# Attention and phase-mixing kernel: 64-column transposes without staging copies, the end of batch 0 in token pieces, batch 3's loads behind one gate, and a channel product ahead of each theta

## The chip, the core and the metric

The kernel runs on one core of one Trainium2 chip. A core has five engines with instruction streams of their own: PE (TensorE: matrix products and transposes into PSUM), DVE (VectorE), ACT (ScalarE), POOL (GpSimd, which here only issues loads) and SP (SyncE, which here issues stores and transposing DMAs). They wait for one another through semaphores; each runs its own instructions in order. Sixteen DMA engines move the data.

The metric is the time of one execution on the device in microseconds. Before the change it is 174.78 us, the median of six runs (174.43 to 175.14).

## The reference

Inputs are q, k, v of shape (4, 8, 768, 64) in float32 (batch, heads, tokens, head width) and the weights of a mixing layer. Reduced to what is computed:

```python
scores = q @ k.T / sqrt(64)
keep   = (pos_k < 8) | ((0 <= rel) & (rel < 96))      # rel = pos_q - pos_k
scores = where(keep, scores - slope[h] * dist, -1e9)  # dist = rel, or 96 for far global keys
x      = softmax(scores) @ v                          # heads side by side: (4, 768, 512)

theta  = x @ w_theta
y      = w_tok_r @ (x * cos(theta)) + w_tok_i @ (x * sin(theta))   # over tokens
u      = x + y
out    = u + relu(u @ w_ch)                            # over channels
```

Every token attends to the eight first ("global") tokens and to the 96 latest ones.

## The kernel before

**Tiles.** 768 tokens are six tiles of 128 (`NT`), 512 channels four groups of 128 (`NC`), eight heads four pairs (`NP`). A pair's two heads of width 64 fill the 128 partitions of qT and kT; their score products use 64 rows of the array each (L295). A pair has three chunks of scores, two key tiles each; each key tile meets its own and the next query tile. The eight global keys are kept by copying them over the first columns of a second key tensor, kG (`kglob`, L214), and likewise vG for v (`vglob`).

**One batch.** (1) Loads: q, k (`qk`) and v (`vn`) from HBM, cast to bf16 by POOL's DMAs. (2) q and k are transposed to qT and kT. Batches 0, 1 and 2 do it on PE, from `qkn`, a copy of qk in which the two heads of a pair lie side by side, so that six transposes of 128 columns make one PSUM tile, which ACT (kT) or DVE (qT) copies out. The copies into qkn are `cast0` (L198, batch 0) and `prep_copy` (L229, batches 1 and 2). Batch 3 does it with transposing DMAs from SP (`prep_dma`), for which its q and k are loaded token-wise, one DMA a head (L82). (3) `scores` and `score_exp` (L302): exp on ACT; the bias is a PE product in batch 0 (`score_bias`) and a product with a table, `etab`, on DVE in the others. (4) `values` (L352) makes x of a pair, with a reciprocal and a multiply on DVE (L360, L362), and `xtrans` makes xT: on PE in batch 0, with an SP DMA (L366) in the others. (5) `theta` (L389) needs all four groups of xT; sine and cosine on ACT (L395), zr and zi on DVE (L398, `zri`). (6) `mix` (L409): 12 products of 512 columns a token tile, then u on DVE (L414). (7) `utrans` makes uT (PE in batch 0 and for the last tile, SP's DMA at L423 else), and `chan` (L434) is four products, one DVE instruction for o_sb (L440) and a store.

**Order.** Batch 0's attention and theta are written out by hand for PE, DVE, ACT, POOL and SP (`manual_schedule`, from L504 to L575). After it, `weave` lays batch b's mixing and batch b+1's attention into one another by weights; in batch 0 the side work, whose first pieces are the transposes of batch 1, begins after 0.3 of the mixing. From there a planner orders each engine's instructions by its own costs, mostly as written; anchors (`behind`) keep the side work from running ahead. The last tile of batch 3 is by hand again.

**Where batches meet.** `order` (L587) holds what runs between two batches: the first four half-steps of theta (`th[:4]`), two of the channel products left from the batch before, `th[4:]`, the rest. Theta's half-steps take channel groups 0 to 2 first and group 3 last.

**Load queue.** POOL issues, in this order: batch 0 (pair 1, half of v, pairs 2 and 3, the other half), the weights, batch 1's q, k, v, batch 2's q, k and, in the weave, v; then the first four heads of batch 3, and behind a one-element copy that waits for the last xT of batch 1 (`load_behind`, L457) its other four heads and its v. The qk and vn buffers are two each, so batch 2 reuses batch 0's and batch 3 batch 1's.

The softmax here doesn't subtract the row's maximum and nothing guards it: scores larger than these inputs give would overflow.

## Time and profile before

| Quantity | Value |
|---|---|
| Median of six runs | 174.78 us (174.43 to 175.14) |
| The profiled execution, its own time | 174.41 us |
| Span of its instructions | 172.4 us |
| Instructions | 3627 |
| HBM read, written | 25.69 MB, 6.29 MB |
| DVE copies into qkn, batches 1 and 2 (L229) | 16, 340 ns each |
| PE transposes from qkn (L204, L244) | 48 and 96, of 128 columns |
| First product of mixing (L409) | 33.04 us |
| Gate of batch 3's loads (L457) | 73.02 us |

Times within the profile count from the start of the span. PE's busy share is no measure of its work: a product of 512 columns is shown with some 380 ns, though the next one starts 216 ns later. Busy shares are averages over stages with different limits; which wait ends last in a stage is read from the chain of work that ended last, which is followed back from the last instruction through what released each one. A row of a timeline gives start, length, engine, line, operation, written and read tiles, and in brackets the idle time before it with what ended it.

### The profile page before, as it was taken

What the parts mean: (1) busy time and instruction counts of PE and PEld (TensorE: products, weight loads), DVE (VectorE), ACT (ScalarE), POOL (GpSimd) and SP (SyncE); (2) the same over time, 40 slices, a digit from 0 to 9 for tenths busy, and PEclk for the clock granted to TensorE, in tenths of its full rate; (3) what the DMA queues carried; (4) which work ended last, traced back from release to release, by engine and by line L of the source; (5) the groups of instructions that cost most, each with busy time, mean ns of one, the idle gap of its engine ahead of it and who ended that gap; (6) DMA issues with size and microseconds to landing.
All of it is one profiled execution on the core that took longest, in us unless ns stands there. A gap on an engine that the chain in (4) does not pass through costs nothing.

```text
span 172.4 us, 3627 instructions
## 1 busy us (share of the span) xinstructions
PE 159.3 (92%) x1457; PEld 84.7 (49%) x1482; DVE 127.7 (74%) x288; ACT 99.1 (58%) x124; POOL 37.4 (22%) x45
## 2 busy tenths in 40 slices
PE   6789878999999999999999998999999989999991
PEld 1355655455755566544454563444554634444440
DVE  7578965678999999998587587597786838724443
ACT  2479676999497595489834730989348318500010
POOL 8974456005371010099000000000000000000000
PEclk9999999999999999999999999999999999999999
DMA  4999999999999999799999797787138571323335
GB/s 157 184 193 178 211 207 209 205 204 171 160 204 175 167 156 165 124 94 157 214 143 111 158 161 165 137 152 223 30 76 116 133 171 41 142 41 102 100 93 183
DMA packets 75088, 25.92 MB, mean 150 GB/s; under 512 B 63168, under 2 KB 72128, under 8 KB 75072
## 3 DMA queue, kind: packets, MB, share of 16 engines
q0 software_dynamic: 45680, 12.45, 78.9%
q1 hardware_dynamic: 28976, 12.72, 34.4%
q10 hardware_dynamic: 416, 0.52, 0.9%
q8 instruction: 11, 0.18, 0.4%
q14 instruction: 5, 0.04, 0.1%
HBM read 25.69 MB, written 6.29 MB: 186 GB/s over the span
## 4 chain that ended last, share of the span: by engine, by line
PE 49%; DMA 22%; DVE 19%; POOL 5%; issue 2%; ACT 1%; SPq 0%; DVEq 0%; POOLq 0%
PE ps L409 27%; DMA qk<-in_k_dram 11%; PE ps L434 9%; DMA w_nat<-in_moe_w_tok_r_dram 7%; PE pb L295 4%; PE pb L352 3%; PE pb L389 3%; DVE qT L249 3%; POOL qk L73 3%; DVE e L312 2%; PE ps L389 2%; DVE qkn L229 2%; DVE o_sb L440 2%; POOL vn L88 2%; DMA kT<-qk 2%
## 5 line engine op out<-in xcount | busy, mean ns | idle before, releaser
L409 PE MATMUL ps<-zri,w_tokT 128*128 128x512 bf16 x271 | 67.4, 380 | 1.5 <-issue 0.5
L302 ACT ACTIVATE e<-pb 128x1024 bf16<-128x1024 f32 (+1 forms) x48 | 43.6, 958 | 22.4 <-PE pb L295 22.2
L409 PEld LDWEIGHTS <-w_tokT 128*128 128x128 bf16 x288 | 26.1, 98 | 29.0 <-issue 1.0
L414 DVE TENSOR_TENSOR u<-x_sb,ps 128x512 bf16<-128x512 bf16 x24 | 16.4, 682 | 14.6 <-PE ps L409 12.7
L434 PE MATMUL ps<-w_ch_bf,uT 128*128 128x512 bf16 x94 | 23.9, 379 | 0.3 <-DVE u L414 0.2
L398 DVE TENSOR_TENSOR zri<-x_sb,cs 128x512 bf16<-128x512 bf16 x48 | 17.9, 417 | 8.0 <-ACT cs L395 7.7
L440 DVE SCALAR_TENSOR_TENSOR o_sb<-ps,u 128x512 f32<-128x512 f32 (+1 forms) x25 | 16.5, 661 | 3.1 <-PE ps L434 3.1
L395 ACT ACTIVATE cs<-pb,halfpi 128x1024 bf16<-128x1024 f32 x8 | 8.9, 1115 | 15.8 <-PE pb L389 15.8
L312 DVE TENSOR_TENSOR e<-e,etab 128x1024 bf16<-128x1024 bf16 (+1 forms) x24 | 14.7, 615 | 3.4 <-ACT e L302 3.4
L295 PE MATMUL pb<-qT,kT 64*128 64x128 bf16 x224 | 15.9, 223 | 0.8 <-ACT kT L211 0.3
L389 PE MATMUL pb<-w_theta_bf,xT 128*128 128x512 bf16 x62 | 15.0, 379 | 1.2 <-DMA xT<-x_sb 1.1
L295 PEld LDWEIGHTS <-kT 64*128 64x128 bf16 x224 | 9.0, 95 | 14.2 <-issue 13.0
L389 PEld LDWEIGHTS <-xT 128*128 128x128 bf16 x96 | 9.1, 98 | 12.0 <-DMA xT<-x_sb 2.1
L428 ACT COPY uT<-ps 128x512 bf16<-128x512 bf16 x7 | 4.1, 587 | 18.6 <-PE ps L427 18.6
L352 PEld LDWEIGHTS <-e 128*128 128x128 bf16 x352 | 12.7, 97 | 3.2 <-issue 1.2
L434 PEld LDWEIGHTS <-uT 128*128 128x128 bf16 x96 | 8.9, 98 | 10.0 <-ACT uT L428 0.3
L88 POOL DMA_DIRECT2D vn<-in_v_dram x5 | 9.6, 1928 | 11.9 <-DVE vn L68 10.3
L295 PE MATMUL pb<-qT,kG 64*128 64x128 bf16 x128 | 12.0, 221 | 0.3 <-DVE kG L220 0.3
L362 DVE TENSOR_TENSOR x_sb<-pb,rec 128x768 bf16<-128x768 f32 x12 | 11.4, 948 | 0.3
L315 DVE TENSOR_TENSOR e<-e,etab 128x1024 bf16<-128x1024 bf16 x12 | 8.2, 684 | 2.8 <-ACT e L302 2.8
L352 PE MATMUL pb<-vn,e 128*128 128x65 bf16 x168 | 9.6, 193 | 0.2 <-DVE x_sb L362 0.2
L251 ACT COPY kT<-ps 128x768 bf16<-128x768 bf16 x8 | 6.4, 798 | 5.0 <-PE ps L244 5.0
(74 smaller groups left out, 205.3 us busy)
## 6 DMA issues: line engine op xcount, KB each, us to landing
out_dram<-o_sb SPq DMA_DIRECT2D x23, 256.0 KB, 2.4
vn<-in_v_dram POOLq DMA_DIRECT2D x3, 768.0 KB, 22.8
qk<-in_q_dram POOLq DMA_DIRECT2D x2, 768.0 KB, 20.8
qk<-in_k_dram POOLq DMA_DIRECT2D x2, 768.0 KB, 23.4
w_nat<-in_moe_w_tok_r_dram POOLq DMA_DIRECT2D x3, 384.0 KB, 13.9
w_nat<-in_moe_w_tok_i_dram POOLq DMA_DIRECT2D x3, 384.0 KB, 14.9
vn<-in_v_dram POOLq DMA_DIRECT2D x2, 384.0 KB, 8.9
qk<-in_q_dram POOLq DMA_DIRECT2D x8, 96.0 KB, 9.0
```

Source lines behind the costliest of these rows:

```text
L88: nc.gpsimd.dma_start(out=vn[:, h0:h0 + n, :, 0:D].rearrange("p h t d -> p (h t) d"), in_=v[b, h0:h0 + n].rearrange("h (t p) d -> p (h t) ...
L295: nc.tensor.matmul(pb[:, hh, o:o + T], lhsT=lhsT, rhs=qT[R, (own, nxt)[part]], start=bool(b), stop=bool(b) or (jt == NT - 1 or (j == 1 and ...
L302: ins = nc.scalar.activation(e_c, pb[:, :, 0:n], AF.Exp, scale=scale).ins
L312: nc.vector.tensor_mul(e_c, e_c, tab[:, :, s0:s0 + n // T].rearrange("p a s n -> p a (s n)"))
L352: nc.tensor.matmul(o, lhsT=l_, rhs=r_, start=(i_ == 0), stop=(i_ == len(mms) - 1))
L362: nc.vector.tensor_mul(xv, po4[:, :, :, 0:D], rec.to_broadcast([T, n, NT, D]))
L389: nc.tensor.matmul(pb[j_] if last else pb[:, j_, :], lhsT=xT[:, dc, st(j_)], rhs=w_theta_bf[:, dc, :], start=(dc == 0), stop=(dc == NC - 1))
L398: nc.vector.tensor_mul(zri[b][:, i_, 2 * c + j_, :].rearrange("p (g d) -> p g d", g=NP), xb[:, :, 2 * c + j_, :], cs[:, i_, j_].rearrange( ...
L409: anchor["pe"] = nc.tensor.matmul(ps, lhsT=w_tokT[wi][:, st, tt * T:(tt + 1) * T], rhs=zri[b][:, wi, st, :], start=(st == 0 and wi == 0), ...
L414: anchor["dve"] = nc.vector.tensor_add(u_sb[b, tt].rearrange("p (g d) -> p g d", g=NP), x_sb[b][:, :, tt, :], ps.rearrange("p (g d) -> p g ...
L434: nc.tensor.matmul(ps_c, lhsT=uT[:, dc, :], rhs=w_ch_bf[:, dc, :], start=(dc == 0), stop=(dc == NC - 1))
L440: nc.vector.scalar_tensor_tensor(o_sb[:, cols], in0=ps_c[:, cols], scalar=0.0, in1=u[:, cols], op0=ALU.max, op1=ALU.add)
```

## The change

- Transposes of q and k on PE (`turn`): each head by itself, 64 stationary columns into 64 of the PSUM partitions, straight from qk; twelve in the place of six. The copies of batches 1 and 2 and of batch 0's pairs 1 to 3 go; pair 0 is still cast from float32, into a buffer `qk0`.
- Batch 0 by hand: the bias products of chunks 0 and 1 and one of the eight exp tables stand ahead of the first transposes; pair 0's kG is made on ACT in two pieces; chunk 2 of the scores stands ahead of the values of the pair before; the values and xT of the last pair are made for token tiles 0 to 3 and then 4 and 5; channel groups 0 to 2 of two thetas run before its last xT. `load_qk(0, 4, 2)` stands ahead of the first half of v.
- Batch 3: all eight heads and v are loaded behind the gate.
- `order`: one `chan` ahead of theta, one (in batch 1's case a `utrans`) in the middle, the rest behind.
- The last `chan` writes two PSUM tiles of 256 columns, so that the first half can go on while the second is computed.

```diff
     load_qk(0, 2, 2)
+    load_qk(0, 4, 2)
     load_v(0, 0, 4)
-    load_qk(0, 4, 2)
...
+    def turn(ps, src):
+        for t_ in range(NT):
+            for hh in range(2):
+                nc.tensor.transpose(ps[hh * D:(hh + 1) * D, t_, :], src[:, hh, t_, :], ident)
 
     def turn0(p, i_):
-        qkn = tiles0[p, "n"]
         ps = tiles0[p, i_] = ps_small([T, NT, T], BF)
-        for t_ in range(NT):
-            nc.tensor.transpose(ps[:, t_, :], qkn[:, t_, i_].rearrange("p h d -> p (h d)"), ident)
+        turn(ps, loads[0][0][:, i_, 2 * p:2 * p + 2] if p else qk0[:, i_])
...
-    def prep_copy(b, p):
-        qk = loads[b][0]
-        qkn = qkns[b, p] = att.tile([T, NT, 2, 2, D], BF, name="qkn", bufs=2)
-        with behind("dve"):
-            for i_ in range(2):
-                nc.vector.tensor_copy(
-                    out=qkn[:, :, i_].rearrange("p t h d -> p h t d"), in_=qk[:, i_, 2 * p:2 * p + 2])
-
-    def prep(b, p):
-        if p == 0:
-            prep_copy(b, 0)
-        if p + 1 < NP:
-            prep_copy(b, p + 1)
-        qkn = qkns[b, p]
+    def prep(b, p):
+        qk = loads[b][0]
...
             with behind("pe"):
-                for t_ in range(NT):
-                    nc.tensor.transpose(ps[:, t_, :], qkn[:, t_, i_].rearrange("p h d -> p (h d)"), ident)
+                turn(ps, qk[:, i_, 2 * p:2 * p + 2])
...
     def theta(b, c, j):
+        last0 = [(j_, NC - 1) for j_ in range(2)]
+        part = {0: [(0, dc) for dc in range(NC - 1)],
+                1: [(1, dc) for dc in range(NC - 1)] + last0,
+                2: [(j_, dc) for j_ in range(2) for dc in range(NC - 1)],
+                3: last0}[j]
...
     def chan(b, tt):
         u, uT = u_sb[b, tt], uTs[(b, tt)]
+        parts = 2 if (b, tt) == (B - 1, NT - 1) else 1
+        n = DM // parts
+        pss_c = [ps_small([T, n], FP) for _ in range(parts)]
+        for i_, ps_c in enumerate(pss_c):
+            for dc in range(NC):
+                nc.tensor.matmul(ps_c, lhsT=uT[:, dc, :], rhs=w_ch_bf[:, dc, i_ * n:(i_ + 1) * n],
+                                 start=(dc == 0), stop=(dc == NC - 1))
...
         with tc.issue_after(g):
-            load_qk_tokens(b, H // 2, H // 2)
+            alloc_qk(b)
+            load_qk_tokens(b, 0, H)
             load_all_v(b)
...
+    score_bias(0, 0)
+    score_bias(0, 1)
+    cast0(1, dve, 0)
+    bias_table(0)
+    cast0(1, act, 1)
     turn0(0, 1)
...
+    kglob(0, 0, 0, 1, act)
     score_mms(0, 0, 0)
-    score_mms(0, 0, 1)
+    kglob(0, 0, 1, NT - 2, act)
     score_exp(0, 0, 0)
...
+        score_bias(p, 2)
+        score_mms(0, p, 2)
         if p:
             values(0, p - 1, 0)
             values(0, p - 1, 1)
-        score_bias(p, 2)
-        score_mms(0, p, 2)
...
+    sine_table()
+    xtrans(0, p - 1, dve)
+    values(0, p, 0, 0, 4)
+    values(0, p, 1, 0, 4)
+    trans_w(0, act)
+    theta(0, 0, 2)
+    xtrans(0, p, dve, 0, 4)
+    values(0, p, 0, 4, 6)
+    values(0, p, 1, 4, 6)
+    theta(0, 1, 2)
+    xtrans(0, p, dve, 4, 6)
+    theta(0, 0, 3)
+    theta(0, 1, 3)
+    theta(0, 2, 2)
+    theta(0, 2, 3)
+    for h in range(1, H):
+        bias_table(h)
...
-        order = th[:4] + rest[:2] + th[4:] + rest[2:] if b else []
+        order = rest[:1] + th[:4] + rest[1:2] + th[4:] + rest[2:] if b else []
...
         if b == 0:
             side[:0] = [(0, lambda: load_all_v(2))]
-            side.append((0, lambda: (alloc_qk(3), load_qk_tokens(3, 0, H // 2))))
```

## The prediction, made before the changed kernel was run

> **What bounds the kernel now.** I read the engine totals first, then the chain of work that ended last in order of time, then each engine's timeline around the places that the diff touches.
>
> ```profile
> PE 159.3 (92%) x1457; PEld 84.7 (49%) x1482; DVE 127.7 (74%) x288; ACT 99.1 (58%) x124; POOL 37.4 (22%) x45
> ```
>
> PE looks full, but its ends are modelled, so I count its work from start to start. In the timeline a 512-column product takes 0.216 us, a 128-column transpose 0.056, a 65-column values product 0.029, and two row-tile score products (heads 0 and 1) start together and take 0.057 as a pair.
>
> ```profile
> 9.39 12.42 DMA w_nat<-in_moe_w_tok_r_dram
> ...
> 22.09 19.42 DMA qk<-in_k_dram
> 41.53 0.60 DVE qkn L229 x2
> ...
> 68.23 0.61 DVE u L414
> ...
> 68.88 1.02 PE ps L434 x4
> 69.90 0.34 PE ps L244 x6
> ```
>
> This is the chain, with columns start, length, what. Three regimes stand in it. Until 41.53 us it is the load queue: batch 1's k lands then, and no earlier engine work can move it. From 41.53 to 68.8 the chain is VectorE without a gap: batch 1's attention and batch 2's transposes inside batch 0's mixing. From 68.88 it is TensorE, apart from short waits at each batch's theta. PE's own demand in 41.5 to 68.9, counted from the weight loads of each line at the prices above, is 22.7 us, and 26 changes of tile shape at 0.09 (next fence) make 25.1 of 27.4 us: PE is idle for only 2.3 us there. So VectorE bounds that stretch, but PE is the next bound close behind.
>
> ```profile
> 80.03 1.02 PE L409 MATMUL ps<-zri,w_tokT 128*128 128x512 bf16 x4
> 80.98 0.34 PE L295 MATMUL pb<-qT,kT 64*128 64x128 bf16 x6
> ...
> 81.39 0.22 PE L295 MATMUL pb<-qT,kG 64*128 64x128 bf16 x2
> 81.54 0.82 PE L409 MATMUL ps<-zri,w_tokT 128*128 128x512 bf16 x3
> ```
>
> Columns: start, length, engine and line. Four mix products from 80.03 should end their issue at 80.89; the row-tile products start at 80.98. The last row-tile pair from 81.39 should be through at 81.45; mixing starts at 81.54. So each change between the full array and row tiles costs 0.09 us.
>
> **The copies go, the transposes double.** Batches 1 and 2 lose the copies into qkn:
>
> ```profile
> L229 DVE COPY qkn<-qk 128x768 bf16<-128x768 bf16 x16 | 5.0, 340 | 0.0
> ```
>
> Thirteen of the sixteen start in 41.5 to 68.9 and hold the chain for about 0.27 us each: 3.5 us off VectorE, which then needs 23.9 of 27.4 us and stops being the bound. In exchange each of the 16 PSUM tiles gets 12 transposes with 64 stationary columns, not 6 with 128. No row of before is column-tiled. Lower bound: the two heads run side by side as the row-tile pairs do, 6 x 0.056 = 0.34 us, nothing added. Upper bound: one after the other, 12 x 0.056 = 0.67 us, 0.34 more a tile. To both come changes of tile shape: putting column tiles where the transposes stand in the timeline adds nine pairs of changes (two neighbours are row-tile scores already), 9 x 0.19 = 1.7 us. [...] The row on the other side: 65-column products with a full 128-column load each issue every 0.029 us, so today's loads are hidden completely[...]. By the row the stretch needs 25.1 + 1.7 = 26.8 of 27.4 us on PE[...]. I take the row, as the nearest measured tiling, and allow 1.2 us of idle PE instead of 2.3, since chains of copies remain: 28.0 against 27.4, **+0.6 us**.
>
> **Batch 0 by hand.** The six casts of its pairs 1 to 3 (L198, 0.27 to 0.35 us each) leave VectorE; three blocks of column tiles add 3 x 0.19 = 0.56 us to PE. Scores of chunk 2 now stand ahead of the values of the pair before, which should return most of the ACT waits at 15.85, 20.57 and 24.36 (0.28, 1.19, 0.85 us): estimate 1.2 us. At the end the values of the first four token tiles need only chunks 0 and 1, and six products each of two thetas run before the last xT; from the last exp (25.17) to the first mix product (33.04) it is 7.87 us today, and ACT's sines pace what follows: estimate 0.9 us. The two extra reciprocals and multiplies fall into VectorE's 2.32 us wait before 30.93; without it they would cost about 0.8. The start is near zero: the four bias products (0.43 each, 6.82 to 8.66) move into PE's 1.63 us idle, but hold the first transposes to about 6.2 instead of 5.56, and kG's copies go to ACT, idle for 1.85 us; between -0.5 and +0.6, I take 0. The early bias_table(0), 0.7 us on ACT from 4.4, delays ACT's cast (5.00) by 0.1 and shortens the later run of eight tables; the earlier pair-2 load puts v behind 384 KB, with vG at 13.26 leaving 2.7 us after v's landing at 10.6. Both are nothing. Together mixing starts 1.2 - 0.56 + 0.9 = 1.5 us earlier. But the transposes of batch 1 wait for k at 41.53, where PE already waits 0.14 us. Only mix products that the planner pulls ahead of that wait keep the gain; unknown, between 0 and 1.5, I take half, **-0.7**.
>
> **Theta.** One chan (4 x 0.216 = 0.86 us) now stands in front.
>
> ```profile
> 105.06 1.46 PE L389 MATMUL pb<-w_theta_bf,xT 128*128 128x512 bf16 x6
> 107.16 2.33 PE L389 MATMUL pb<-w_theta_bf,xT 128*128 128x512 bf16 x10 [0.64 <-DMA xT<-x_sb]
> ...
> 114.06 1.02 PE L409 MATMUL ps<-zri,w_tokT 128*128 128x512 bf16 x3 [0.25 <-DVE o_sb L440]
> ...
> 139.20 1.46 PE L389 MATMUL pb<-w_theta_bf,xT 128*128 128x512 bf16 x6
> 141.15 2.33 PE L389 MATMUL pb<-w_theta_bf,xT 128*128 128x512 bf16 x9 [0.48 <-DMA xT<-x_sb]
> ```
>
> Six products from 105.06 are issued by 106.36, the seventh starts at 107.16: 0.80 us lost waiting for xT; from 139.20 the same reading gives 0.65. Both are under 0.86, and the uT needed was issued at 132.32 for the later one, so chan covers them whole. Its o_sb (0.61 us on VectorE) also leaves the row of zri products that PE waits for before 114.06 (0.41 from start to start). Sum **-1.85**. Batch 1's theta waits for nothing and gains nothing; were a chan late, it would hold theta by that much.
>
> **Batch 3's loads.** Eight q/k issues (L82, 0.83 us each) move from 46.12 to 62.8 behind the gate:
>
> ```profile
> 73.02 0.21 POOL L457 COPY gate<-xT 1x1 bf16<-1x1 bf16 x1 [10.19 <-DMA xT<-x_sb]
> ...
> 79.99 2.27 POOL L88 DMA_DIRECT2D vn<-in_v_dram  x1
> 84.22 5.91 SPq L423 DMA_TRANSPOSE uT<-u x2
> DMA to landing us min/median/max: 2.4/2.4/8.5
> ```
>
> These are POOL's and SP's queues, and the landing times of uT. POOL then issues 16 loads, and v queues behind them: 8 x 0.83 = 6.6 us later, at 86.6, landing 12.9 us later near 99.5. SP's first transposes of batch 3 (96.47) need heads 0 and 1, there by about 82; vG at 106.07 waits for v, 6 us covered. What is late next is uT: the one issued at 84.22, beside v, took 8.5 us to 92.7, and its chan started at 93.02. With v later, the uT issued near 89 lands between 91.3 (2.4 us) and 99.5, its chan standing at 97.67: 0 to 1.9 us on PE. [...] the row of 8.5 says otherwise and decides, but it is one of 17. I take **+0.4**. In 46 to 63 the freed queue has no waiter: v2, q2 and k2 were ahead of these loads.
>
> **Tail.** The last chan becomes two PSUM halves.
>
> ```profile
> 166.94 1.89 PE L434 MATMUL ps<-w_ch_bf,uT 128*128 128x512 bf16 x8
> ...
> 168.87 0.76 DVE L440 SCALAR_TENSOR_TENSOR o_sb<-ps,u 128x256 f32<-128x256 f32 x2 [0.17 <-PE ps L434]
> ```
>
> The pair of L440 that ends the kernel starts when all four last products are done. Halved, the first can start 0.43 us earlier, behind the o_sb that occupies VectorE from 168.01 to 168.6; the second then starts when the first does today and ends some 0.25 us earlier: **-0.25**. PE's 8 products of 256 columns stand between the rows for 128 and 512 and sum to the same.
>
> **The sum.** +0.6 - 0.7 - 1.85 + 0.4 - 0.25 = -1.8 us. The profiled execution took 174.41 us, its span 172.4 and 2.0 around it, so 172.6; the median shown, 174.78, lies 0.37 above that execution, so I carry the difference to it: **173.0 us**.
>
> **The rivals.** (A) The sum above, chance 0.46; its own range 171.8 to 174.3, from a middle stretch between -0.2 and +1.5 us and the ends for uT and for batch 0.
>
> (B) Slower: the two column tiles of a pair do not overlap. Place: PE between 41.5 and 73. Twelve transposes at 0.056 make 14 x 0.34 = 4.7 us more in the stretch, so 31.5 us of work plus 0.3 idle against 27.4: +4.4 in place of +0.6; two more tiles behind it add 0.7; in batch 0 six tiles add 2.0, and mixing starts 0.5 later instead of 1.5 earlier. Together 4.4 + 0.7 + 0.5 - 1.85 + 0.4 - 0.25 = +3.9, 178.7 us. For it: [...] PE's 2.3 us as the only room. Against it: row-tile pairs that start together. It decides from where the 16 x 6 pairs eat 1.8 us: 19 ns each, a pair at 0.075 us. Chance 0.26, from 174.8 up.
>
> (C) The later loads cost their full 1.9 us, because uT waits out all of v: 174.5 us, no measurable change. For it the landing of 8.5 us; against it the one of 88.94, which was 4.1 us (issue to 93.1), v's last packets having gone by then. Chance 0.12.
>
> (D) More gain: the planner fills the wait for k, and VectorE's relief lets PE run nearly without idle: 0 for the stretch, -1.5 for batch 0, 0 for uT, so -3.6 and 171.2 us. For it: today's planner already moves single mix products between transposes (44.23, two of them). Against it: it put the transposes exactly at their written place at 41.55. Chance 0.16.
>
> **How the numbers follow.** The time is A's. About 0.3%, 0.5 us, is what a measurement of this kernel can tell from no change. A gives 0.41 faster and 0.05 same; D 0.16 faster; C 0.05 faster, 0.04 same, 0.03 slower; B 0.01 faster, 0.25 slower. Sum: faster 0.63, same 0.09, slower 0.28. For 8 in 10 the range takes D whole, A and C, and B as far as pairs of some 0.095 us: 170.8 to 177.0.
>
> **What the profile after would show.** Transposes as 64-column tiles: pairs starting together and 0.34 us for twelve (A) or 0.056 apart and 0.67 (B). L229 and L198 for pairs 1 to 3 gone, and the chain in 42 to 69 on PE rather than DVE. First transposes of batch 1 still at about 41.5, with a PE wait ahead of them of up to 1.5 us, or more mix products there. The seventh theta product of batches 2 and 3 without a wait. POOL's v issue near 86, and chan's second uT of batch 1 with or without a wait on PE. My number fails most easily on the price of a pair; next on an order by the planner that I can't see, which could put a transpose or a values group behind a wait on any engine.

## The result and the profile after

The changed kernel takes 176.22 us (median of 29 executions), the kernel before on the same chips 175.01 (64): a ratio of 1.0073, 95% interval 1.0058 to 1.0088. By the ratio it is 1.3 us slower; the forecast was 173.0 us, faster. The profiled execution of the changed kernel took 176.59 us, its span is 174.6.

The column tiles first. The groups of instructions by line, then the chain that ended last in order of time (start, length, what):

```profile
L200 PE MATMUL ps<-ident,qk 128*64 128x128 bf16 x288 | 11.4, 228 | 0.6 <-DVE qk L195 0.4
```

```profile
41.76 0.46 PE ps L200 x12
42.23 0.53 PE ps L200 x12
...
55.42 1.95 ACT e L291 x2
57.39 0.69 DVE e L303
...
68.39 0.79 PE ps L200 x24
...
73.00 0.86 PE ps L431 x4
73.86 1.29 PE pb L383 x6
```

Twelve 64-column transposes take 0.46 us with a change of tile shape, 24 take 0.79. In the trace each pair of heads starts 56 ns after the one before it, so the two heads run side by side, and VectorE no longer holds the chain without a gap. But the chain did not get shorter: mixing of batch 1 starts at 81.02 us, 1.0 later than before.

The end of batch 0, in ScalarE's timelines (start, length, engine, line, operation; in brackets the idle time before it and what ended it), before and then after:

```profile
24.36 0.81 ACT L302 ACTIVATE e<-pb 128x768 bf16<-128x768 f32 x1 [0.85 <-PE pb L295]
...
29.79 1.11 ACT L395 ACTIVATE cs<-pb,halfpi 128x1024 bf16<-128x1024 f32 x1 [1.55 <-PE pb L389]
```

```profile
14.33 1.02 ACT L291 ACTIVATE e<-pb 128x1024 bf16<-128x1024 f32 x1 [0.63 <-PE pb L281]
...
18.57 1.02 ACT L291 ACTIVATE e<-pb 128x1024 bf16<-128x1024 f32 x1 [0.63 <-PE pb L281]
...
24.18 0.81 ACT L291 ACTIVATE e<-pb 128x768 bf16<-128x768 f32 x1 [0.59 <-PE pb L281]
...
30.18 1.11 ACT L389 ACTIVATE cs<-pb,halfpi 128x1024 bf16<-128x1024 f32 x1 [2.80 <-PE pb L383]
```

The last exp comes only 0.18 us earlier, though VectorE has lost six casts and the first exp came 0.42 earlier (9.39 to 8.97). The first sine comes 0.39 later. The sines run back to back from there, so zri is complete at 36.72 (36.31 before) and u of the first token tile follows at 37.56 (37.17). The first mix product does stand earlier (32.13 for 33.04), but the group that it belongs to then waits for zri.

Around batch 2's theta, first POOL and SP (their issues), then TensorE:

```profile
72.70 0.18 POOL L453 COPY gate<-xT 1x1 bf16<-1x1 bf16 x1 [31.17 <-DMA xT<-x_sb]
...
86.75 2.34 POOL L88 DMA_DIRECT2D vn<-in_v_dram  x1
```

```profile
85.22 6.45 SPq L417 DMA_TRANSPOSE uT<-u  x2
91.85 1.29 SPq L355 DMA_TRANSPOSE xT<-x_sb  x1
94.00 1.23 SPq L417 DMA_TRANSPOSE uT<-u  x1
95.68 2.72 SPq L355 DMA_TRANSPOSE xT<-x_sb  x1
98.49 0.53 SPq L438 DMA_DIRECT2D out_dram<-o_sb  x1
...
107.46 1.24 SPq L355 DMA_TRANSPOSE xT<-x_sb  x1
```

```profile
107.45 1.51 PE L383 MATMUL pb<-w_theta_bf,xT 128*128 128x512 bf16 x6
110.27 2.33 PE L383 MATMUL pb<-w_theta_bf,xT 128*128 128x512 bf16 x10 [1.31 <-DMA xT<-x_sb]
...
142.43 1.46 PE L383 MATMUL pb<-w_theta_bf,xT 128*128 128x512 bf16 x5
144.12 2.33 PE L383 MATMUL pb<-w_theta_bf,xT 128*128 128x512 bf16 x10 [0.23 <-DMA xT<-x_sb]
```

v is issued at 86.75, as predicted, and lands at 100.8. SP's transposes beside it land late (the xT issued at 91.85 after 8.7 us, the next after 7.7), SP, which issues one after another (each issue from 98.49 to 107.46 starts within 0.11 us of the end of the one before), comes late with what follows, and the last x of batch 2 is issued at 107.46 and lands at 110.2. So the seventh theta product waits 1.5 us, in spite of the channel product in front.

### The profile page after: what moved, and what is told of

It reads as the page before. It is cut to its first block, busy times and chain, and to the rows that moved or that the text cites. A ratio compares the mean times of both kernels' runs of the same rounds, so it can differ in the third digit from the quotient of the medians.

```text
span 174.6 us, 3902 instructions
## 1 busy us (share of the span) xinstructions
PE 160.2 (92%) x1604; PEld 84.6 (48%) x1630; DVE 122.9 (70%) x270; ACT 99.4 (57%) x127; POOL 37.8 (22%) x45
## 4 chain that ended last, share of the span: by engine, by line
PE 49%; ACT 16%; DMA 15%; DVE 12%; POOL 4%; issue 2%; SPq 1%; DVEq 0%; ACTq 0%; POOLq 0%
PE ps L403 23%; PE ps L431 7%; ACT e L291 7%; DMA vn<-in_v_dram 7%; ACT cs L389 6%; DMA uT<-u 5%; PE pb L383 5%; PE pb L340 3%; PE pb L281 3%; PE ps L200 3%; POOL qk L73 2%; DMA xT<-x_sb 2%; PE ps L383 2%; DVE x_sb L351 2%; DMA kT<-qk 2%
## 5 line engine op out<-in xcount | busy, mean ns | idle before, releaser
L403 PE MATMUL ps<-zri,w_tokT 128*128 128x512 bf16 x272 | 68.3, 380 | 2.2 <-DVE zri L392 0.7
L291 ACT ACTIVATE e<-pb 128x1024 bf16<-128x1024 f32 (+1 forms) x48 | 43.4, 953 | 18.5 <-PE pb L281 18.1
L431 PE MATMUL ps<-w_ch_bf,uT 128*128 128x512 bf16 (+1 forms) x96 | 24.3, 371 | 0.4 <-DMA uT<-u 0.2
L281 PE MATMUL pb<-qT,kT 64*128 64x128 bf16 x224 | 15.2, 219 | 2.7 <-DVE qT L211 1.3
L422 ACT COPY uT<-ps 128x512 bf16<-128x512 bf16 x7 | 4.1, 588 | 18.5 <-PE ps L421 18.5
L200 PE MATMUL ps<-ident,qk 128*64 128x128 bf16 x288 | 11.4, 228 | 0.6 <-DVE qk L195 0.4
L281 PE MATMUL pb<-qT,kG 64*128 64x128 bf16 x128 | 11.5, 216 | 0.4 <-DVE kG L222 0.4
L200 PEld LDWEIGHTS <-qk 128*64 128x64 bf16 x288 | 9.2, 114 | 4.6 <-issue 2.3
```

Of the source, the lines that this page charges most:

```text
L200: nc.tensor.transpose(ps[hh * D:(hh + 1) * D, t_, :], src[:, hh, t_, :], ident)
L281: nc.tensor.matmul(pb[:, hh, o:o + T], lhsT=lhsT, rhs=qT[R, (own, nxt)[part]], start=bool(b), stop=bool(b) or (jt == NT - 1 or (j == 1 and ...
L291: ins = nc.scalar.activation(e_c, pb[:, :, 0:n], AF.Exp, scale=scale).ins
L403: anchor["pe"] = nc.tensor.matmul(ps, lhsT=w_tokT[wi][:, st, tt * T:(tt + 1) * T], rhs=zri[b][:, wi, st, :], start=(st == 0 and wi == 0), ...
L431: nc.tensor.matmul(ps_c, lhsT=uT[:, dc, :], rhs=w_ch_bf[:, dc, i_ * n:(i_ + 1) * n], start=(dc == 0), stop=(dc == NC - 1))
```

## The experiments

A name with b_ is the kernel before with the edit, one with a_ the changed kernel with it. A ratio is to the kernel before on the same chip, with its 95% interval; 0.001 of it is 0.175 us. The other columns are from one profiled execution each, in us: when TensorE starts the first transpose of batch 1 and the first mix product of batches 1, 2 and 3. In seven of these executions TensorE's clock was granted at half for 3.4 us in batch 0 (a_early_k, a_gate_earlier, a_gate_v_first, a_old_end, a_v_before, b_chan_bias_early, a_bias_late), so that their columns can be late. Comments in the diffs are added.

| Kernel | Ratio | Batch 1's transposes | Mixing 1 | Mixing 2 | Mixing 3 |
|---|---|---|---|---|---|
| before | 1 | 41.55 | 80.03 | 114.06 | 147.63 |
| after | 1.0073 (1.0058, 1.0088) | 41.69 | 81.02 | 115.89 | 149.75 |
| b_chan_first | 0.9917 (0.9891, 0.9943) | 41.60 | 80.42 | 113.38 | 146.72 |
| b_chan_tail | 0.9918 (0.9888, 0.9947) | 41.80 | 80.54 | 113.52 | 146.96 |
| b_coltile_prep | 1.0008 (0.9993, 1.0024) | 41.34 | 80.82 | 114.70 | 148.28 |
| b_chan_coltile | 0.9957 (0.9941, 0.9972) | 41.22 | 81.40 | 114.36 | 147.79 |
| b_loads_gate | 1.0263 (1.0220, 1.0307) | 41.74 | 79.81 | 119.47 | 153.29 |
| b_gate_chan | 1.0085 (1.0050, 1.0120) | 41.59 | 79.92 | 115.54 | 148.98 |
| a_loads_early | 1.0023 (1.0001, 1.0045) | 41.61 | 81.05 | 114.36 | 147.97 |
| a_gate_earlier | 1.0032 (1.0008, 1.0056) | 41.79 | 80.91 | 113.88 | 147.89 |
| a_gate_v_first | 1.0024 (1.0006, 1.0041) | 41.94 | 81.07 | 114.31 | 148.14 |
| a_early_copies | 1.0000 (0.9976, 1.0025) | 42.67 | 81.32 | 115.02 | 148.47 |
| a_early_k | 1.0029 (1.0003, 1.0055) | 41.95 | 81.32 | 114.44 | 148.75 |
| a_old_end | 1.0029 (1.0013, 1.0045) | 41.67 | 81.72 | 114.75 | 148.59 |
| a_v_before | 1.0028 (1.0008, 1.0047) | 43.52 | 82.81 | 115.96 | 149.60 |
| a_front_back | 1.0004 (0.9984, 1.0024) | 42.10 | 81.65 | 115.54 | 149.21 |
| b_chan_bias_early | 0.9938 (0.9913, 0.9963) | 41.95 | 80.45 | 113.48 | 146.92 |
| a_bias_late | 1.0072 (1.0046, 1.0097) | 41.99 | 81.27 | 115.11 | 148.83 |
| b_chan_fill | 1.0045 (1.0023, 1.0068) | 41.53 | 80.20 | 114.87 | 149.10 |
| a_fill | 1.0016 (0.9995, 1.0038) | 41.80 | 81.08 | 114.40 | 147.70 |

### The loads of batch 3

The first edit, and the reverse of it for a_loads_early:

```diff
         with tc.issue_after(g):
-            load_qk_tokens(b, H // 2, H // 2)
+            alloc_qk(b)
+            load_qk_tokens(b, 0, H)
             load_all_v(b)
...
-            side.append((0, lambda: (alloc_qk(3), load_qk_tokens(3, 0, H // 2))))
```

> The kernel before with one edit: all eight heads of batch 3 and its v are loaded behind the gate. The instruction orders of PE and SP are those of before. Theory Q (the late v load fills the DMA engines from about 84 to 98 us, SP's transposes of batch 1's u and batch 2's x back up behind it, the last xT of batch 2 comes about 3 us late and theta and kG wait): slower by 1.0 to 2.0 us, ratio 1.006 to 1.011, theta's wait in batch 2 grows from 0.8 to 2 us or more. Theory T (the loss is TensorE's column tiles in 41 to 73 us, the loads cost at most the wait for one uT): within 0.4 us of before, ratio 0.998 to 1.002.

> The changed kernel with one edit undone: the first four heads of batch 3 are loaded at the end of batch 0's side work again, the other four and v behind the gate. Orders of PE and SP as in the changed kernel. Theory Q: it returns 1.5 to 2.3 us, that is 0.992 to 0.999 of the kernel before; theta of batch 2 waits less than 0.3 us. Theory T: no change against the changed kernel, 1.005 to 1.009 of before.

The loads cost more by themselves than theory Q had it: 1.0263, some 4.6 us. Taken out of the changed kernel they give back 0.0050, 0.87 us: less than theory Q's 1.5 to 2.3, more than theory T's nothing. Theory Q's other clause held, theta of batch 2 has no wait:

```profile
107.45 3.62 PE L383 MATMUL pb<-w_theta_bf,xT 128*128 128x512 bf16 x16
```

The two profiled executions are further apart than the medians, 1.8 us of span: that of a_loads_early took 174.79 us, 0.5 under its median, that of the changed kernel 0.4 over its own. The work of b_loads_gate around batch 2's theta, as busy time of each engine in two stretches (the granted clock is the number ahead of the last two), and TensorE's timeline:

```profile
104.00:107.80 3.80, 1.44 (x7) 0.48 (x5) 1.31 (x4) 0.00 (x0) 0.00 (x0) 1.00 1.31 147
107.80:114.60 6.80, 4.89 (x12) 1.76 (x13) 2.36 (x6) 2.03 (x2) 0.00 (x0) 0.50 0.88 207
```

```profile
104.85 0.59 PE L389 MATMUL pb<-w_theta_bf,xT 128*128 128x512 bf16 x2
109.71 5.61 PE L389 MATMUL pb<-w_theta_bf,xT 128*128 128x512 bf16 x14 [4.26 <-DMA xT<-x_sb]
```

TensorE waits 4.26 us for x. Within this wait, at 107.8 us, the granted clock falls to half. It stays there for 6.8 us, and 14 products take 5.61 us where 16 take 3.62 at full clock. With the channel product in front as well:

> The kernel before with all loads of batch 3 behind the gate and one channel product ahead of each theta. The gate alone cost 4.7 us, most of it because TensorE stood still for several us at the theta of batch 2 and then ran at half clock. Theory Q (the channel product and the later transposes shorten that standstill below what lowers the clock, as in the changed kernel): 175.0 to 176.3 us, no stretch of half clock, mixing of batch 2 at 115 to 116 us. Rival (the standstill still lowers the clock): 178 us or more, with a stretch of half clock after 107 us.

No half clock there, in none of 9 executions (b_loads_gate: a mean clock of 0.99 or less in all 6), theta's wait is 1.20 us, and the ratio 1.0085: the channel product prevents the drop. The time, 176.72 us, is 0.4 above what was expected. With the channel product in front the loads cost 1.0085 - 0.9917 = 0.0168, 2.9 us, twice what it gains. So the same move costs 4.6, 2.9 and 0.87 us in three kernels; why least in the changed one was not traced.

Then two ways of having v earlier behind the gate:

```diff
-            order.insert(0, lambda: load_behind(3, xT_sb[1][0:1, NC - 1, 0:1]))
+            order.insert(0, lambda: load_behind(3, xT_sb[1][0:1, NC - 2, 0:1]))
```

```diff
             alloc_qk(b)
-            load_qk_tokens(b, 0, H)
             load_all_v(b)
+            load_qk_tokens(b, 0, H)
```

> The changed kernel with the gate of batch 3's loads on the third x of batch 1 in place of the last, some 4 us earlier; the same 16 loads of q and k and then v stand behind it. Theory Q (what costs is how late these loads run: they saturate the queue from 84 to 99 us, hold SP's transposes of batch 2's x back, and the last x reaches theta 3 us late): v's issue near 82 to 83 us, the last x of batch 2 lands near 107 to 108 us, theta of batch 2 without a wait, 175.1 to 175.5 us, as with the loads in their old place. Rival (the number of loads behind one gate costs, not their time): the wait at theta of batch 2 stays over 1 us, 176.0 to 176.5 us.

> The changed kernel with v of batch 3 ahead of its q and k behind the gate. Theory v (the lateness of v alone, as the prediction's sum had it): v lands near 92 us as before, the uT and x transposes of 90 to 98 us run freely, 175.1 to 175.5 us. Theory Q (any load that keeps the software queue saturated from 84 to 99 us does it, and the same bytes stand behind the gate): the last x of batch 2 still lands near 110 us, 176.0 to 176.6 us, or later, since q and k of the first pair then come late for SP's own transposes near 99 us.

```profile
72.88 2.22 POOL L88 DMA_DIRECT2D vn<-in_v_dram  x1 [0.56 <-DVE kG L222]
```

```profile
107.12 3.89 PE L383 MATMUL pb<-w_theta_bf,xT 128*128 128x512 bf16 x16
...
114.31 1.03 PE L403 MATMUL ps<-zri,w_tokT 128*128 128x512 bf16 x4
```

Those are POOL and TensorE of a_gate_v_first: the sixteen theta products run nearly through (3.89 us; 3.62 without any wait), mixing 2 starts at 114.31. Both kernels come to the ratio of a_loads_early, with all 16 loads of q and k still behind the gate; in a_gate_earlier the clause on theta's wait held too. So theory v holds and theory Q, in the form that any load in that window does it, falls: v's lateness is what the gate costs.

### The channel product and the tail

```diff
-        order = th[:4] + rest[:2] + th[4:] + rest[2:] if b else []
+        order = rest[:1] + th[:4] + rest[1:2] + th[4:] + rest[2:] if b else []
```

> The kernel before with one edit: one channel product ahead of each theta. Both theories: the waits of 0.80 and 0.65 us at theta are covered, and zri comes sooner in batch 2; faster by 1.0 to 1.85 us, ratio 0.989 to 0.994. If it gains less than 0.7 us, my reading of those waits was wrong.

> The kernel before with one channel product ahead of each theta and the last channel product in two PSUM halves. Theory Q (each of the two gains by itself: 1.4 us for the channel product, as the run with it alone gave, and 0.25 us for the tail): 173.2 us, ratio 0.990, the same start of the last mixing as with the channel product alone (146.7 us) and the end 0.25 us nearer to it. Rival (the tail's halves buy nothing, because the last output write is fixed by something else): 173.45 us, ratio 0.992.

The second adds the two halves of the last `chan`. TensorE at the thetas of batches 2 and 3 in b_chan_first:

```profile
105.61 1.03 PE L434 MATMUL ps<-w_ch_bf,uT 128*128 128x512 bf16 x4
106.47 3.62 PE L389 MATMUL pb<-w_theta_bf,xT 128*128 128x512 bf16 x16
...
113.38 1.03 PE L409 MATMUL ps<-zri,w_tokT 128*128 128x512 bf16 x4
...
139.81 3.62 PE L389 MATMUL pb<-w_theta_bf,xT 128*128 128x512 bf16 x16
```

Sixteen products in one piece: the wait is gone, at batch 2's theta too. The channel product gives 0.0083, 1.45 us, and b_chan_first (173.46 us, one line changed) is the fastest of all. The tail gives nothing (0.9918 for 0.9917); its rival, that the last output write is fixed by something else, was right. The end of VectorE and the last write (KB, us to landing) in b_chan_first and then in b_chan_tail:

```profile
167.96 0.76 DVE L440 SCALAR_TENSOR_TENSOR o_sb<-ps,u 128x256 f32<-128x256 f32 x2 [0.17 <-PE ps L434]
out_dram<-o_sb ACTq DMA_DIRECT2D x1, 128.0 KB, 1.8
```

```profile
167.34 1.35 DVE L442 SCALAR_TENSOR_TENSOR o_sb<-ps,u 128x512 f32<-128x512 f32 x3 [0.49 <-PE ps L437]
out_dram<-o_sb ACTq DMA_DIRECT2D x1, 128.0 KB, 2.1
```

From mixing 3 on, VectorE ends after 21.99 us in the first and 21.73 in the second: the 0.25 us came there. But the last write lands in 2.11 us for 1.84, and so after 23.87 us in both. Why it takes longer was not tried.

### Column tiles

`prep` and `turn` as in the change, for batches 1 and 2 alone, without and with the channel product; a_early_copies is the reverse, a_loads_early with the copies back.

> The kernel before with one edit: batches 1 and 2 transpose from qk in 64-column tiles, without the copies into qkn; batch 0 as before. Theory Q: the stretch from 41.5 to 73 us grows by the changes of tile shape less what VectorE's relief gives, 0 to 0.9 us slower, ratio 1.000 to 1.005. Theory T: 1.0 us slower or more, ratio 1.006 to 1.012.

> The kernel before with one channel product ahead of each theta and with column-tile transposes for batches 1 and 2. Alone, the first gave 1.4 us and the second cost 0.3 us, while it started the mixing of batch 1 0.8 us later: the waits for x at the thetas of batches 2 and 3 took the rest in. Theory P (with the channel product in front those waits are gone, TensorE bounds every stage, and column tiles then cost their whole 0.8 us): 174.1 to 174.4 us, mixing of batch 1 near 81.1 us. Rival (the two add up): 173.5 to 173.8 us.

> The changed kernel with batch 3's loads where they were and with the copies into qkn and the full-array transposes back in batches 1 and 2; batch 0's order by hand, the channel product ahead of theta and the tail stay. Theory Q (column tiles in batches 1 and 2 are worth about nothing, as the run with them alone gave; what eats the channel product's gain is batch 0's new order, which ends against the landing of k and leaves the scores of batch 1 later): 174.9 to 175.3 us, mixing of batch 1 at 80.7 to 81.1 us. Rival R (column tiles cost more beside batch 0's new order, because four blocks of transposes now stand ahead of the first scores of batch 1 on TensorE): mixing of batch 1 at about 79.5 us and 173.5 to 173.9 us in all.

Alone, column tiles cost 0.0008, about nothing; with the channel product 0.9957 - 0.9917 = 0.0040, 0.70 us, as theory P had it. The mechanism that P named isn't seen: TensorE's waits for x in 80 to 150 us are 1.0 us in b_coltile_prep and 1.1 before, so the waits took in little. The profiled executions show 0.8 and 1.0 us at mixing 1. In a_early_copies v's second half landed 0.4 us later than in the changed kernel's profiled execution and held ScalarE by 1.59 us at 22.37, so its columns are not a clean comparison; its ratio fits theory Q. Less than a_loads_early by 0.0023, it puts column tiles at 0.4 us in the changed kernel.

### Batch 0

What is left is a_loads_early against b_chan_coltile: 1.0023 - 0.9957 = 0.0066, 1.15 us for batch 0's order (the tail being worth nothing). A second pair, without column tiles in batches 1 and 2 and on one chip, says the same: a_early_copies less b_chan_tail is 0.0082, 1.4 us. Behind batch 0 every engine has the same instructions in the same order in a_loads_early and b_chan_coltile, the tail aside. First the landing of k, which the prediction had as the floor for batch 1's transposes:

```diff
     load_w()            # without the last two token weights and w_ch
     load_all_qk(1)
+    load_w_rest()       # these three
     load_all_v(1)
```

> The changed kernel with batch 3's loads where they were, and with q and k of batch 1 issued ahead of the last two token weights and the channel weights, so that k lands some 6 us earlier (estimate 36 us). Theory Q (batch 0's gain of 0.9 us is lost at the landing of k near 42 us): TensorE's wait ahead of the first transposes near 41.7 us goes, mixing of batch 1 starts 0.9 to 2 us earlier than the 81.06 of the same kernel without this edit, and the whole takes 173.3 to 174.4 us. Rival R (the order of transposes and scores in batch 0's mixing eats the gain, k or no k): the wait goes but mixing of batch 1 still starts at 80.7 us or later, 174.9 to 175.3 us.

k of batch 1 lands at 35.5 us for 42.1, and nothing is gained. The first transposes start 9.56 us behind the first mix product, in all three of this kernel (32.39 to 41.95), a_loads_early (32.05 to 41.61) and the changed kernel (32.13 to 41.69). The landing was no floor; the rival holds.

Next the end of the last pair as before (values, x and theta whole), the first half of v ahead of pair 2 again, and both together with the bias products at their old place:

```diff
-    xtrans(0, p - 1, dve)
-    values(0, p, 0, 0, 4)
-    values(0, p, 1, 0, 4)
+    xtrans(0, p - 1, act)
+    values(0, p, 0)
+    values(0, p, 1)
     trans_w(0, act)
-    theta(0, 0, 2)
-    xtrans(0, p, dve, 0, 4)
...
+    xtrans(0, p)
+    for c in range(NT // 2):
+        theta(0, c, 0)
+        theta(0, c, 1)
```

> The changed kernel with batch 3's loads where they were, and with the end of batch 0 as before: the values of the last pair whole, its x transposed and copied whole, each theta's eight products in one go. Theory E (the split end delays the sines: in the changed kernel six products of each theta are done early, but the first theta's last two products come after the split copies, at 29.5 us, and the first sine at 30.2 us against 29.8 us before): the first sine starts near 29.6 us, batch 1's first transposes 0.4 to 0.6 us earlier than the 41.61 of the same kernel with the split end, and the whole takes 174.7 to 174.9 us against 175.3. Rival (the split end does bring the sines forward and something else in batch 0 takes the time): the first sine later than 30.1 us, 175.6 us or more.

> The changed kernel with batch 3's loads where they were, and with the first half of batch 0's v loaded ahead of q and k of pair 2 again. Theory V (v's landing at 13.2 us in place of 10.6 us holds VectorE at vG by 0.9 us and again by 0.7 us at the second half, and the score chain behind it): vG starts near 12.4 us without a wait, the last exp of batch 0 starts 0.5 to 1.2 us earlier than the 24.10 of the same kernel without this edit, and the whole takes 174.1 to 174.8 us. Rival (VectorE's wait is slack, ScalarE and TensorE set the pace there): last exp within 0.2 us, the whole 175.1 to 175.4 us.

> The changed kernel with batch 3's loads where they were and, in batch 0, the bias products, the first half of v and the end of the last pair as before; the order of scores and values in the loop, kG's copies on ScalarE and column tiles stay. Theory D: 174.2 to 174.7 us, spread under 1 us; what then stays above the 173.5 us of the channel product alone is the column tiles. Rival (the order of scores and values is what costs): 175.0 us or more.

ScalarE in a_old_end:

```profile
24.75 0.81 ACT L291 ACTIVATE e<-pb 128x768 bf16<-128x768 f32 x1 [0.59 <-PE pb L281]
...
30.16 1.11 ACT L389 ACTIVATE cs<-pb,halfpi 128x1024 bf16<-128x1024 f32 x1 [1.55 <-PE pb L383]
```

From the last exp's end to the first sine it is 4.60 us here, 4.62 in the kernel before, 5.19 in the changed kernel. So the split end does delay the sines by 0.6 us, but with that given back the ratio stays. (Mixing 1 can't be read there: the half clock made the last exp of this profiled execution 0.65 us late.) In a_v_before vG no longer waits for v's first half as it did (11.80 us, 0.17 of wait), and the ratio stays too; its columns are late by half clock from 15.2 to 18.6 us and by a wait of TensorE for pair 2's k, 1.74 us. With three pieces undone, a_front_back comes to 1.0004, not to the 0.9957 of column tiles and channel product: 0.8 us remain. It keeps the new loop, kG's copies on ScalarE, the early exp table and batch 0's own column tiles, none of which was taken out by itself.

Nor was the second half of v, which lands at 18.6 us in the changed kernel for 17.4 before. In six of its ten variants it lands at 18.5 to 19.2, a_v_before and a_front_back among them, in every variant of the kernel before at 16.8 to 17.8; vG waits for it by 0.66 us in the changed kernel and 1.27 in a_early_copies. How much of the 1.15 us this is, no run shows.

One more thing is read in the order, and was not tried. TensorE in batch 0's loop, before and after:

```profile
16.71 0.59 PE L275 MATMUL pb<-dist,diag 128*128 128x512 bf16 x2
17.23 0.23 PE L295 MATMUL pb<-qT,kT 64*128 64x128 bf16 x2
...
17.81 0.84 PE L204 MATMUL ps<-ident,qkn 128*128 128x128 bf16 x12 [0.18 <-DVE qkn L198]
```

```profile
16.80 0.86 PE L200 MATMUL ps<-ident,qk 128*64 128x128 bf16 x24
17.59 0.60 PE L261 MATMUL pb<-dist,diag 128*128 128x512 bf16 x2
18.13 0.23 PE L281 MATMUL pb<-qT,kT 64*128 64x128 bf16 x2
```

The new loop puts the transposes of the pair after next ahead of the bias and scores of chunk 1, for which ScalarE waits 0.63 us at 18.57. Before, they stood behind. From the first exp to the end of the last it is 15.78 us before and 16.02 after, and 16.5 in a_front_back, in one profiled execution each.

### Half clock in batch 0

Of the first eight profiled executions of the changed kernel and its variants, five had half clock in batch 0. The bias products alone in b_chan_first, and put back in a_loads_early:

```diff
     diagonals(0)
+    score_bias(0, 0)
+    score_bias(0, 1)
     cast0(0, 1, dve, 0)
...
     kglob(0, 0)
-    score_bias(0, 0)
-    score_bias(0, 1)
```

> The kernel before with one channel product ahead of each theta and, of batch 0's new order, only the four bias products of the first two chunks ahead of the casts. Theory D ([...] the wait for qT and kT that then follows, some 1.3 us near 7 us, lets the clock drop to half near 8 us in part of the executions, as in five of the changed kernel's eight variants that were profiled): 173.6 to 174.2 us with a wide spread, up to 175 us; in the profile a granted clock of 0.5 near 8 to 12 us, or none with the first exp near 8.7 us. Rival (the half clock comes from something else in batch 0's order): 173.0 to 173.4 us with a spread of under 1 us, the first exp 0.3 to 0.6 us earlier than 9.38.

> The changed kernel with batch 3's loads where they were, and with the four bias products of batch 0's first two chunks back at their old place, ahead of the first scores. Theory D (their early place is what lets the clock drop): no granted clock under 0.9 in 0 to 25 us, the first exp near 9.2 us, the median 174.6 to 175.0 us with a spread of under 1 us. Rival (the half clock comes from the rest of batch 0's order): 175.2 to 175.7 us, spread over 1.5 us, half clock in the profile as before.

The granted clock of b_chan_bias_early in 40 slices of 4.3 us, in tenths:

```profile
PEclk9969999999999999999999999999999999999999
```

The early bias products bring it about: a mean granted clock under 0.993 in 4 of 9 executions of b_chan_bias_early and in none of 8 of b_chan_first. With the products late it is 1 of 10 for 8 of 14 in a_loads_early; the profiled execution of a_bias_late was the one that had it. They aren't enough by themselves: a_v_before keeps them early, with a wait of 1.26 us behind them, and has it in 1 of 22. And it isn't what costs: b_chan_bias_early loses 0.0021, within the intervals, and a_bias_late is slower than its base, not faster. Both numbers expected of a_bias_late were missed. Its profile has the loss at two waits for transposing DMAs (0.7 us for a uT, 0.3 for an x); why the old place costs more here was not traced.

### Instruction fetches

Those waits led to the last pair. The DMA table has a queue for instructions, with packets of 16 KB (q8: 12 packets, 0.20 MB in the changed kernel). The traces before and after show one for 241 and 240 instructions of TensorE on average, from one to the next 125 to 358. Behind 108 us, when the loads are done, SP issues 428 transposing DMAs in the 20 traces of this study. In the time of 82 of them an instruction fetch starts: 46 of these take over 3.9 us, the other 36 take 2.4 to 3.8. Of the 346 without one none takes over 3.9, and nine in ten take 2.4 to 2.9. In b_chan_first the fetches start at 99.4, 115.8, 127.7 and 142.0 us, in a_loads_early at 99.2, 116.0, 128.2 and 138.7. The last one there meets the x that theta of batch 3 waits for.

```diff
+    def fill(n):
+        ps = ps_small([T, 64], FP)
+        for _ in range(n):
+            nc.tensor.matmul(ps, lhsT=zero[:, 0:T], rhs=zero[:, 0:64], start=True, stop=True)
...
     warm(6)
+    fill(30)            # b_chan_fill; a_fill: fill(40) behind turn0(0, 0)
```

Nothing reads what `fill` writes; it only moves TensorE's later instructions by two places a product, a weight load and the product itself (the six products of `warm` stand in the trace as 6 and 6).

> The kernel before with one channel product ahead of each theta, and with 30 products of 64 columns of zeros on TensorE behind the first warming products of batch 0, in its wait of 1.6 us there. They move all later instructions of TensorE by 60 places. Theory F: the instruction fetch of 142.0 us comes near 138.6 us and holds the x issued near 135.5 us: it lands in 4.3 us and not 2.7, theta of batch 3 waits 0.2 to 0.7 us, the whole takes 173.7 to 174.2 us. Rival (the fetches don't touch the transposes): landing 2.7 us, no wait at theta of batch 3, 173.3 to 173.5 us.

> The changed kernel with batch 3's loads where they were, and with 40 products of 64 columns of zeros on TensorE behind the first transposes of batch 0, where it waits 1.3 us for qT and kT (near 7 us). They do two things: TensorE doesn't stand still there, and all its later instructions stand 80 places further on. Theory F (instruction fetches of 16 KB, [...] hold single transposes by DMA; in the changed kernel one falls at 138.7 us, into the x that theta of batch 3 waits for): the fetch near 134 us, the x issued near 136.4 us lands in 2.7 us and not 4.4, no wait at theta of batch 3, from mixing 2 to mixing 3 33.4 us. Theory D (the standstill lowers the clock): no granted clock under 0.9 in 0 to 25 us. Both: 174.3 to 174.8 us. Rival (neither matters): 175.2 to 175.6 us and the wait at theta of batch 3 stays.

The DMA view of b_chan_first from 135 to 137.5 us, with no packet of instructions, and of b_chan_fill from 137 to 139.5 (issues: KB each left out, median us to landing last):

```profile
q1 hardware_dynamic: 770, 0.33, 52.1%
...
xT<-x_sb SPq DMA_TRANSPOSE x1, 2.7
```

```profile
q8 instruction: 1, 0.02, 3.1%
...
xT<-x_sb SPq DMA_TRANSPOSE x1, 4.2
```

VectorE and TensorE of b_chan_fill around mixing 2, and TensorE at batch 3's theta:

```profile
112.51 0.29 DVE L223 COPY kG<-kT 128x512 bf16<-128x512 bf16 x1 [4.12 <-DMA kT<-qk]
```

```profile
114.87 1.02 PE L414 MATMUL ps<-zri,w_tokT 128*128 128x512 bf16 x4 [1.22 <-DVE o_sb L445]
...
143.48 2.33 PE L394 MATMUL pb<-w_theta_bf,xT 128*128 128x512 bf16 x10 [0.61 <-DMA xT<-x_sb]
```

One fetch (3.1% of 16 engines in 2.5 us is 1.24 us on one of them) holds the x by 1.5 us, theta waits 0.61; another, at 109.8, holds a kT (VectorE waits 4.12 us for it, 2.31 in b_chan_first), behind it zri and o_sb on VectorE, and mixing 2 waits 1.22. Up to mixing 1 this kernel is as fast as b_chan_first (80.20 for 80.42). In all it loses 0.0128, 2.2 us, by 30 products that stand where TensorE is idle: more than theory F expected. The reverse in a_fill:

```profile
140.80 3.62 PE L388 MATMUL pb<-w_theta_bf,xT 128*128 128x512 bf16 x16
```

The fetch starts at 135.7, the x lands in 3.0 us, theta of batch 3 has no wait and mixing 2 to 3 takes 33.30 us for 33.61; no execution of 14 had the low clock. Its ratio is 1.0016 for 1.0023, a gain that the intervals don't separate from none. Both, the fetch there and the low clock, are gone from this kernel, and that gave next to nothing; 1.0016 - 0.9957 = 0.0059, 1.0 us, of batch 0's order stays open. The profiled executions of a_fill and b_chan_coltile have spans of 172.5 and 172.6 us and neither has a transposing DMA over 3.9 us behind 108 us, so they don't show it. What tells the medians apart is in executions without a profile: those of a_fill lie between 174.04 and 175.96 us, those of b_chan_coltile, on another chip, between 173.82 and 174.87. The fastest are close, the spread is not.

The kernels of the table have their fetches at different places. By b_chan_fill a difference between two of them can hold some 2 us that belong to the fetches and not to the edit.

## Why the prediction was wrong

The sum was -1.8 us; the differences of ratios make +1.27. They add up by construction, and each is known to some 0.5 us by the intervals.

| Step | Predicted | Measured | From |
|---|---|---|---|
| Column tiles in the middle stretch | +0.6 | +0.70 | b_chan_coltile less b_chan_first |
| Batch 0 by hand | -0.7 | +1.15 | a_loads_early less b_chan_coltile |
| Theta | -1.85 | -1.45 | b_chan_first |
| Batch 3's loads | +0.4 | +0.87 | after less a_loads_early |
| Tail | -0.25 | 0.0 | b_chan_tail less b_chan_first |

**Batch 0 by hand** is the step that failed: wrong in sign, and 1.85 of the 3.1 us by which the sum missed. The second pair above gives 1.4. Three parts of it did not come. "Should return most of the ACT waits", 1.2 us: the waits behind 12.9 us sum to 2.50 after (0.63, 0.63, 0.65, 0.59) and 2.70 before. The prediction didn't follow where the transposes went in the loop, and it priced the later v at nothing: v lands at 13.2 instead of 10.6, and vG waits 0.88 and 0.66 for its halves, shown by the trace; the first half is worth nothing by a_v_before (1.0028 for 1.0023), the second was not tried. "ACT's sines pace what follows: estimate 0.9 us" named the right pace and got the wrong sign, -0.39: two of theta's eight products now come behind the split copies. "The transposes of batch 1 wait for k at 41.53", by which half of the gain was kept, was refuted by a_early_k. What the runs show in place of the gain is a loss of 1.15 us; 0.39 of later sines and 0.24 of a longer exp loop are seen in the trace, and giving back the sines did not move the ratio (1.0029 for 1.0023). Why the order costs 1.15 us stays open.

**Batch 3's loads** had the mechanism, v later, and its times (issue 86.6 for 86.75, landing 99.5 for 100.8), which a_gate_v_first confirms. The size was off by a factor of two because uT alone was named as late next. Behind uT on SP's queue stand the x of batch 2; theta waits for the last of them, and SP issues in order. The row of 8.5 us, which decided there, was right: the uT issued at 89.94 landed at 99.06, though its chan waited only 0.22 us for it.

**Theta** gave 1.45 of 1.85 us. All the waits of the sum, zri's with them, are gone in b_chan_first's trace: from theta's first product, or the channel product now ahead of it, to mixing 2 the same 36 products take 7.77 us for 9.00, and those to mixing 3 7.77 (138.95 to 146.72) for 8.43, together 1.89 less. What is missing was lost elsewhere in the profiled executions, 0.39 us before mixing 1 and 0.43 between mixing 2 and batch 3's theta, and was not followed. In the changed kernel the late x makes the cover too short by 1.5 us.

**Column tiles** were right: pairs start 56 ns apart, beside 57 ns for the row-tile pair of the prediction's lower bound. That the sum of the step fits is partly luck: between the first transposes and mixing 1 the changed kernel has 34 changes of tile shape for 26, 0.7 us at 0.09 each, where nine pairs, 1.7 us, were assumed, and VectorE's relief was to pay for 1.1 of them. The result lies in rival B's range and B's mechanism is refuted; rival C's time, 174.5 us, was nearest, and its uT did wait out v, but the wait that counted was theta's. **The tail** shortened VectorE by 0.26 us, as the sum had it; the last write then landed 0.27 us more slowly, a term that the sum didn't have.

## What to carry to other kernels

When a load moves, list everything behind its neighbours on an in-order issuing queue and price the last transfer that an engine waits for, not the first that is late. When stages overlap, follow what paces the next one (here the sines), not the first instruction of it that starts earlier, and write out each reordered loop pair by pair. A difference of 1% between two kernels can come from the instruction count alone (30 products more in b_chan_fill: 1.0045 for 0.9917); before explaining one, see where the instruction packets fall among the transfers that engines wait for, and try a few filler instructions in idle time.

## What the runs showed of the hardware

- An instruction fetch of 16 KB (0.9 to 1.5 us on one DMA engine in the traces before and after) lengthened a transposing DMA in its time from 2.7 us (b_chan_first) to 4.2 (b_chan_fill); 46 of 82 transposes with a fetch in their time took over 3.9 us, none of 346 without. 30 idle-time products that shifted the fetches cost 2.2 us (1.0045 for 0.9917).
- In a wait of 4.26 us TensorE's granted clock fell to half, for 6.8 us (b_loads_gate). In batch 0, a wait of 1.3 us behind early products was followed by 3.4 us of half clock in some executions (by the mean clock 9 of 29 of the changed kernel, 8 of 14 of a_loads_early, 1 of 22 of a_v_before), and in none of 14 where the wait was filled with small products (a_fill).
- Two 64-column transposes in different column tiles ran as a pair every 56 ns (changed kernel). Their weight loads, shown with 110 ns each, started as far apart, and the idle time ahead of all 288 sums to 0.6 us.
- Beside v's load through the software queue (changed kernel), four transposing DMAs issued from 89.94 to 95.68 us landed after 7.2 to 9.1 us for 2.4 to 2.8.
- Where the last three output writes were issued within 0.93 us, the last landed in 1.84 us (b_chan_first); within 0.66 us, in 2.11 (b_chan_tail).
